# Key rows in two runs, values in eight pieces, the second unit's query rows ahead of the first weights, and nine warming products: one change to the opening of a fused attention and expert kernel

## The chip, the cores and the metric

The kernel runs on one core of one Trainium2 chip. The time is the device time of one execution in microseconds (us). Before the change, six runs gave a median of 487.77 us, from 487.45 to 488.29.

A core has five engines that matter here: TensorE (PE in the profile; its weight loads are PEld), VectorE (DVE), ScalarE (ACT), GpSimd (POOL) and SyncE (SP), which does nothing but issue DMAs. SPq and ACTq are the queues on which SP and ACT issue them.

## The reference

Attention first, with features that are products of two sketches of a row; then a mixture of four experts on its output. All is float32.

```
q, k, v: (4 batches, 4 heads, 1088 rows, 32)      S1, S2: (8, 32)
phi(x) = outer(S1 x, S2 x)                         # 64 features per row
kv = sum_s phi(k_s) v_s^T ;  z = sum_s phi(k_s)
attn = phi(q) kv / (phi(q) z + 1e-6)
x = attn, laid out as (4*1088, 4 heads * 32) = (4352, 128)
p = domain_probs / sum(domain_probs)               # (4352, 4)
out = sum_e p[:, e] * (relu(x @ w1[e]) @ w2[e])    # w1: (4,128,1024), w2: (4,1024,128)
```

The sum over the key rows runs over all 1088 of a batch and head, so the order in which they are taken is free, as long as keys and values are taken in the same order.

## The kernel before, in words

**Tiles.** A batch's k lies in SBUF as kn, 128 partitions by 1088 numbers: partition 32h+i holds 34 consecutive rows of head h, 32 numbers each. VectorE turns it in 32x32 blocks into kT, nine key tiles of 128 rows (the last is half full): `key_turn` (L326) turns tiles 0 to 3 with r = 0, 4 to 7 with r = 1, the half tile with r = 2. Before the change a tile of r = 0 takes its four groups of rows 8 rows apart, from the whole length of the partition's line. v comes as vn in four pieces of 1 KB runs, one for each group of 32 partitions, and two small ones for the half tile (`load_v`, L101); ScalarE copies it into vx (`value_copy`, L335). Query rows of a batch are worked on in units; those of batch 0 are 128, 448 and 512 rows, so the second unit is columns 128 to 575 of qn.

**Order.** All instructions are written out by hand in the order of the code; each engine takes its own in that order. `start()` (L674 on) does the first unit: `key_turn` for tiles 0 and 1, for 2 and 3, for r = 1 and r = 2 (VectorE), the query turn, the key products with the sketches (`key_project`, L344), ScalarE's copies of them and of v, feature products on VectorE and GpSimd, `key_sum` (72 products on TensorE), then the first unit's attention. The second unit's query turn (128x256 and 128x192) stands on VectorE ahead of `key_divide`. Then TensorE goes over the steps (L976): four steps per expert, each a first product (xT with w1, `first`, L775) and, two steps later, a second product (hidden units with w2, `second`, L831). Steps 0 to 3 need w1 of expert 0, steps 4 to 7 w1 of expert 1, and so on. Steps of the first 128 rows are short; from about 30 us on TensorE has long products.

**Warming.** `keep_warm(11)` (L192) puts eleven bfloat16 products of constants, 128x512, at TensorE's head; they are used for nothing.

**Loads.** All loads but one go through SP, in this order: S2, k of batch 0 (L99), the first 128 query columns, v (L105 four times, L110 twice), the other 960 query columns, w1 of expert 0 (L130), domain_probs in three and the ends' in two (L151, L156), w2 of expert 0 (L133), then w1 and w2 of experts 1, 2, 3. S1 goes through ACT. The framework gives the DMAs of all queues eight semaphores in turn, so an issue waits until the DMA eight places before it in the program has landed; w1 of expert 0, for instance, waits for the first query columns. Later batches are loaded by `load_batch` (L118) at step 5 and inside `front`, ahead of stores of y to DRAM (L609).

Of the kernel before, what the change touches and what calls it, by code (L numbers as in the profile page):

```python
# [8 lines left out]
F32 = mybir.dt.float32  # L9
# [3 lines left out]
ACTF = mybir.ActivationFunctionType  # L13
# [3 lines left out]
def _ap(t, p0: int, np_: int, off: int, free):  # L17

    p = list(t.ap)[0]
    return bass.AP(t.tensor, t.offset + p0 * p[0] + off, [[p[0], np_]] + [list(d) for d in free])  # L20
# [3 lines left out]
def kernel(  # L24
# [24 lines left out]
    nc = tc.nc  # L49

    P = 128
    HP = 64
    B, H, S, D = q.shape
# [3 lines left out]
    G = S // 32  # L57
# [8 lines left out]
    UNITS = [[P, 448, 512], [512, 320, 256], [448, 512, P], [384, 320, 384]]  # L66
# [6 lines left out]
    cpool = ctx.enter_context(tc.tile_pool(name="const", bufs=1))  # L73
# [10 lines left out]
    def psum(pool, tag):  # L84
        return pool.tile([P, 512], F32, tag=tag, name=tag)


    def load_rows(src, b, name, part=slice(0, S)):

        d = kn if name == "kn" else qn  # L90
        if b not in d:
            d[b] = lpool.tile([P, S], F32, tag=name, bufs=2, name=name)
        c, n = part.start, part.stop - part.start
        base = src.offset + b * H * S * D
        if name == "qn" and b == B - 1:
            for c, n, t in ((0, (G - 4) * D, 0), ((G - 4) * D, 4 * D, S - P)):
                nc.sync.dma_start(d[b][:, c : c + n], bass.AP(src.tensor, base + t * D, [[S * D, H], [n, 32], [1, n]]))
        else:
            nc.sync.dma_start(d[b][:, part], bass.AP(src.tensor, base + c, [[G * D, P], [1, n]]))  # L99

    def load_v(b):  # L101
        t = lpool.tile([P, H * NT * D], F32, tag="vn", name="vn")
        base = v.offset + b * H * S * D
        for a in range(4):
            nc.sync.dma_start(  # L105
                _ap(t, 32 * a, 32, 0, [[8 * D, H], [1, 8 * D]]),
                bass.AP(v.tensor, base + 8 * a * D, [[G * D, 32], [S * D, H], [1, 8 * D]]),
            )
        for a in range(2):
            nc.sync.dma_start(  # L110
                _ap(t, 32 * a, 32, 1024, [[D, H], [1, D]]),
                bass.AP(v.tensor, base + (32 + a) * D, [[G * D, 32], [S * D, H], [1, D]]),
            )
        return t

    kn, qn, vn = {}, {}, {}

    def load_batch(b):  # L118
        load_rows(k, b, "kn")
        vn[b] = load_v(b)  # L120
        load_rows(q, b, "qn")
# [7 lines left out]
    def load_w1(e):  # L129
        nc.sync.dma_start(w1_sb[:, e, :], w1[e])  # L130

    def load_w2(e):
        nc.sync.dma_start(w2_sb[:, e], w2[e].rearrange("(f p) d -> p f d", p=P))  # L133

    load_rows(k, 0, "kn")
    load_rows(q, 0, "qn", slice(0, P))
    vn[0] = load_v(0)


    warm = nc.const_aps.tensor(1.0, (P, 512), BF16)  # L140

    idle = cpool.tile([P, 1], F32, name="idle")
    nc.scalar.activation(idle[:, :], nc.const_aps.tensor(1.0, (P, 1), F32), ACTF.Identity)
    dp = cpool.tile([P, G, E], F32, name="dp")

    ends = cpool.tile([P, 2, E], F32, name="ends")
    e_sum = cpool.tile([P, 2, 3], F32, name="e_sum")
    load_rows(q, 0, "qn", slice(P, S))
    load_w1(0)
    for p0, n, g0, m, t in ((0, 96, 0, G, 0), (96, 32, 0, G - 4, 3 * S), (96, 32, G - 4, 4, B * S - P)):  # L150
        nc.sync.dma_start(  # L151
# [3 lines left out]
    for i, t, g in ((0, 0, G), (1, B * S - P, 4)):  # L155
        nc.sync.dma_start(  # L156
            ends[:, i, :], bass.AP(domain_probs.tensor, domain_probs.offset + t * E, [[g * E, 32], [1, 4 * E]])
        )
    load_w2(0)
    for e in range(1, E):  # L160
        load_w1(e)
        load_w2(e)
# [23 lines left out]
    def keep_warm(n):  # L186

        for _ in range(n):
            wp = psum(ps_h, "h")
            nc.tensor.matmul(wp[:, :], warm[:, 0:P], warm[:, :], start=True, stop=True)  # L190

    keep_warm(11)  # L192


    turn = [0]
# [130 lines left out]
    def key_turn(b, r, t0=0, n=4):  # L326
        if r < 2:
            nc.vector.transpose(
                _ap(kT, 0, P, 512 * r + P * t0, [[P, n], [32, 4], [1, 32]]),
                _ap(kn[b], 0, P, P * r + 32 * t0, [[32, n], [8 * D, 4], [1, 32]]),  # L330
            )
        else:
            nc.vector.transpose(kT[:, 1024:S], kn[b][:, 1024:S])
# [98 lines left out]
    def keys(b):  # L432
        for r in range(3):
            key_turn(b, r)
            yield
        kf = []
        for gi, (pool, tag) in enumerate(((ps_f, "f"), (ps_n, "den"), (ps_n, "num"))):
            kf.append(psum(pool, tag))
            key_project_wide(b, gi, kf[gi])
            if gi:  # L440
                key_add(b, gi - 1, kf[gi - 1])
            yield
        for _ in value_copy(b):
            pass
        for t0, n in ((0, 4), (4, 5)):
            if t0:
                key_add(b, 2, kf[2])
            for p in range(2):
                for x in range(2):
                    key_product(b, t0, n, p, x, nc.vector)  # L450
                    yield
        yield
        yield
        kv = psum(ps_f, "f")
        for p in range(2):
            key_sum(b, p, kv)
            yield
        key_blocks(b, kv)
        yield
# [214 lines left out]
    def start():  # L674
# [4 lines left out]
        for t0 in (0, 2):  # L679
            key_turn(b, 0, t0, 2)  # L680
        for r in (1, 2):
            key_turn(b, r)
# [366 lines left out]
```

## Time and profile before

| | us |
|---|---|
| median of six runs | 487.77 |
| profiled execution | 489.03 |
| its span, first to last instruction | 487.2 |
| time around the span | 1.83 |
| TensorE busy | 481.9 (99%) |
| VectorE busy | 320.9 (66%) |
| ScalarE busy | 246.6 (51%) |
| GpSimd busy | 229.9 (47%) |

A line of the chain of waits reads: start, length, what ran. A line of a timeline reads: start, length, engine, source line, operation, tile written <- tile read, shape, number of instructions merged, and in brackets the idle time before them with what ended it. A line of stages reads: from:to, its length, then each engine's busy time with its number of instructions, the granted TensorE clock, the busy share of the DMA engines and GB/s. A line of DMA issues reads: what, queue, operation, number, KB each, median us from the start of the issue to landing.

### The profile page before, as it was taken

The page shows a single profiled execution, that of the slowest core. Times are in us where ns is not written, and L with a number is a line of the kernel's source. Part 1 is how long each engine was busy: PE and PEld are TensorE (multiplying, and loading weights), DVE is VectorE, ACT ScalarE, POOL GpSimd, SP SyncE. Part 2 cuts the span into 40 slices and gives each one's busy share as a digit, 9 for nine tenths or more (in the row PEclk, how much of TensorE's full clock was granted, in tenths as well). Part 3 has the DMA queues.
Part 4 walks back from the last instruction along what each step waited for, and adds up shares of the span by engine and source line. Part 5 has one row for each costly group of instructions (what it writes and reads, how often), then busy time and mean ns, then how long its engine had stood idle before and what let it go on. Part 6 is the DMA issues. An engine that isn't in the chain of part 4 may idle for free.

```text
span 487.2 us, 11377 instructions
## 1 busy us (share of the span) xinstructions
PE 481.9 (99%) x4551; PEld 363.2 (75%) x4551; DVE 320.9 (66%) x759; ACT 246.6 (51%) x496; POOL 229.9 (47%) x270
## 2 busy tenths in 40 slices
PE   9999999999999999999999999999999999999997
PEld 6865666667777777777777777677777777999997
DVE  6759766585766658476776766668674666665642
ACT  4264464455554456355445545435455545566651
POOL 5172654425445445415455444424555445555571
PEclk9999999999999999999999999999999999999999
DMA  7991041111003123021103100021101200120000
GB/s 218 281 277 32 13 132 39 49 50 46 8 1 114 24 69 93 1 86 24 40 1 129 24 12 2 1 86 24 34 0 56 50 1 0 44 51 8 15 3 18
DMA packets 37772, 26.25 MB, mean 54 GB/s; under 512 B 24824, under 2 KB 34520, under 8 KB 37208
## 3 DMA queue, kind: packets, MB, share of 16 engines
q1 hardware_dynamic: 37704, 25.53, 18.6%
q8 instruction: 36, 0.59, 0.5%
q14 instruction: 16, 0.13, 0.1%
q10 hardware_dynamic: 16, 0.00, 0.0%
HBM read 21.28 MB, written 4.24 MB: 52 GB/s over the span
## 4 chain that ended last, share of the span: by engine, by line
PE 96%; DMA 2%; SPq 1%; issue 0%; DVE 0%
PE h L202 49%; PE o L202 41%; PE f L202 3%; PE den L202 2%; DMA w_sb<-in_moe_w_dram 2%; DMA vn<-in_v_dram 1%; PE num L202 0%; SPq L105 0%; SPq L156 0%; SPq L99 0%; SPq L133 0%; SPq L125 0%; DVE end L856 0%
## 5 line engine op out<-in xcount | busy, mean ns | idle before, releaser
L202 PE MATMUL h<-xT,w_sb 128*64 128x512 f32 (+5 forms) x1424 | 298.9, 491 | 1.2 <-DMA w_sb<-in_moe_w_dram 1.2
L786 DVE SCALAR_TENSOR_TENSOR hid<-h,hid 128x256 f32<-128x256 f32 (+6 forms) x432 | 203.8, 472 | 143.3 <-ACT hid L817 134.9
L817 ACT ACTIVATE hid<-h 128x512 f32<-128x512 f32 (+3 forms) x288 | 158.3, 550 | 192.5 <-PE h L202 146.2
L202 PE MATMUL o<-hid,w2s 128*64 128x256 f32 (+3 forms) x1152 | 223.9, 355 | 0.0
L202 PEld LDWEIGHTS h<-xT,w_sb 128*64 128x64 f32 x1424 | 146.5, 137 | 51.4 <-issue 7.5
L202 PE MATMUL o<-hid,w_sb 128*64 128x256 f32 (+3 forms) x864 | 183.7, 355 | 0.0
L202 PEld LDWEIGHTS o<-hid,w2s 128*64 128x64 f32 x1152 | 132.3, 137 | 28.8
L930 POOL TENSOR_TENSOR ev<-yz,sh 64x256 f32<-64x256 f32 (+3 forms) x72 | 48.6, 675 | 159.9 <-ACT sh L933 157.2
L202 PEld LDWEIGHTS o<-hid,w_sb 128*64 128x64 f32 x864 | 100.6, 137 | 24.9 <-issue 5.8
L918 POOL TENSOR_TENSOR yz<-ev 128x512 f32<-128x512 f32 (+3 forms) x36 | 41.8, 1160 | 60.5 <-ACT ev L921 60.3
L930 POOL TENSOR_TENSOR ct<-ev 128x512 f32<-128x512 f32 (+3 forms) x36 | 42.5, 1181 | 2.8
L930 POOL TENSOR_TENSOR total<-total,ct 128x512 f32<-128x512 f32 (+3 forms) x27 | 31.9, 1182 | 2.1
L930 POOL TENSOR_TENSOR ct<-ct,gate 128x512 f32<-128x512 f32 (+3 forms) x27 | 31.8, 1176 | 2.1
L501 DVE TENSOR_TENSOR qp<-qa,qb 64x512 f32<-64x512 f32 (+5 forms) x44 | 30.0, 683 | 1.0
L920 ACT COPY ev<-o 128x512 f32<-128x512 f32 (+3 forms) x36 | 19.4, 538 | 12.8 <-PE o L202 12.3
L202 PE MATMUL o<-w_sb,hid 128*64 128x128 f32 x256 | 21.4, 273 | 0.0
L921 ACT COPY ev<-o 128x512 f32<-128x512 f32 (+3 forms) x36 | 19.4, 538 | 2.0
L202 PEld LDWEIGHTS o<-w_sb,hid 128*64 128x64 f32 x256 | 17.2, 137 | 1.6 <-issue 0.9
L809 ACT ACTIVATE hid<-h 128x256 f32<-128x256 f32 x23 | 8.4, 384 | 19.3 <-PE h L202 18.9
L391 DVE TENSOR_TENSOR kp<-fs 128x256 f32<-128x256 f32 (+1 forms) x24 | 16.7, 698 | 0.1
L933 ACT COPY sh<-yz 64x256 f32<-64x256 f32 (+3 forms) x36 | 13.7, 380 | 1.6 <-POOL yz L918 0.8
L202 PEld LDWEIGHTS den<-kvx,qp 128*64 128x64 f32 x240 | 12.3, 137 | 2.6 <-issue 0.5
(129 smaller groups left out, 247.0 us busy)
## 6 DMA issues: line engine op xcount, KB each, us to landing
w_sb<-in_moe_w_dram SPq DMA_DIRECT2D x8, 512.0 KB, 7.8
gate<-gates SPq DMA_DIRECT2D x4, 1024.0 KB, 4.6
kn<-in_k_dram SPq DMA_DIRECT2D x4, 544.0 KB, 7.3
vn<-in_v_dram SPq DMA_DIRECT2D x16, 128.0 KB, 3.5
gate<-gates SPq DMA_DIRECT2D x2, 896.0 KB, 6.2
qn<-in_q_dram SPq DMA_DIRECT2D x2, 544.0 KB, 3.9
out_dram<-ob SPq DMA_DIRECT2D x16, 64.0 KB, 2.0
qn<-in_q_dram SPq DMA_DIRECT2D x2, 480.0 KB, 4.0
```

The costliest lines, as they stand in the source:

```text
L202: nc.tensor.matmul(out(s), weights(s), moving(s), **flags)
L391: eng.tensor_tensor(out=_ap(kps[b], 0, P, 256 * t0 + P * p + 64 * x, [[256, n], [32, 2], [R, 4], [1, R]]), in0=_ap(src, 0, P, off + 4 * x, ...
L501: nc.vector.tensor_tensor(out=qp[p][64 * x : 64 * x + 64, 0:n], in0=qa[64 * p : 64 * p + 64, 0:n], in1=qb[64 * p : 64 * p + 64, 0:n], op=A ...
L786: nc.vector.scalar_tensor_tensor(out=out, in0=src, scalar=0.0, in1=in1, op0=ALU.max, op1=ALU.subtract)
L809: nc.scalar.activation(hd[:, 0 : 2 * n], hp[:, 0 : 2 * n], ACTF.Relu)
L817: nc.scalar.activation(hd[:, n * j : n * j + n], hp[:, 0:n], ACTF.Relu)
L918: add = lambda out, in0, in1, op=ALU.add: nc.gpsimd.tensor_tensor(out=out, in0=in0, in1=in1, op=op)
L920: nc.scalar.copy(_ap(ev, 0, P, 0, [[2 * w, 2], [1, w]]), _ap(a0, 0, P, 0, two))
L921: nc.scalar.copy(_ap(ev, 0, P, w, [[2 * w, 2], [1, w]]), _ap(a1, 0, P, 0, two))
L930: add = lambda out, in0, in1, op=ALU.add: nc.gpsimd.tensor_tensor(out=out, in0=in0, in1=in1, op=op)
L933: nc.scalar.copy(sh[HP:P, 0:w], yz[0:HP, 0, 0:w])
```

## The change

Key tiles 0 to 3 are made of the first 16 rows of each partition's line and tiles 4 to 7 of the next 16, so each of them needs only one half of the line; k of batch 0 comes in two loads, columns 0 to 511 and 512 to 1087. v comes in eight pieces of 512-byte runs, four for each half, and the two small ones, for every batch. For batch 0 the first 128 query columns and one piece of v are issued on ACT, behind the activation `idle`, which moves ahead of the loads. Of the other query columns, the second unit's 448 stay ahead of w1 of expert 0, now behind all of v; the last 512 move behind w2 of expert 0. Nine warming products instead of eleven.

SP's order in batch 0 is now: S2, k (512 columns), k (576), v x7, small v x2, q (448), w1 of expert 0, domain_probs x3, ends x2, w2 of expert 0, q (512), w1 of expert 1, w2 of expert 1 and so on. Of the seven pieces of v on SP, the fifth waits for k's first load, the sixth for its second, the seventh for the query columns issued on ACT.

```diff
-    def load_rows(src, b, name, part=slice(0, S)):
+    def load_rows(src, b, name, part=slice(0, S), engine=nc.sync):
...
-            nc.sync.dma_start(d[b][:, part], bass.AP(src.tensor, base + c, [[G * D, P], [1, n]]))
+            engine.dma_start(d[b][:, part], bass.AP(src.tensor, base + c, [[G * D, P], [1, n]]))
...
-        for a in range(4):
-            nc.sync.dma_start(
-                _ap(t, 32 * a, 32, 0, [[8 * D, H], [1, 8 * D]]),
-                bass.AP(v.tensor, base + 8 * a * D, [[G * D, 32], [S * D, H], [1, 8 * D]]),
-            )
+        for r in range(2):
+            if b == 0 and r:
+                load_rows(q, 0, "qn", slice(0, P), nc.scalar)
+            for a in range(4):
+                (nc.scalar if b == 0 and r and a == 0 else nc.sync).dma_start(
+                    _ap(t, 32 * a, 32, P * r, [[8 * D, H], [1, P]]),
+                    bass.AP(v.tensor, base + (16 * r + 4 * a) * D, [[G * D, 32], [S * D, H], [1, P]]),
+                )
...
-    load_rows(k, 0, "kn")
-    load_rows(q, 0, "qn", slice(0, P))
-    vn[0] = load_v(0)
-    warm = nc.const_aps.tensor(1.0, (P, 512), BF16)
     idle = cpool.tile([P, 1], F32, name="idle")
     nc.scalar.activation(idle[:, :], nc.const_aps.tensor(1.0, (P, 1), F32), ACTF.Identity)
+    for part in (slice(0, 512), slice(512, S)):
+        load_rows(k, 0, "kn", part)
+    vn[0] = load_v(0)
+    warm = nc.const_aps.tensor(1.0, (P, 512), BF16)
...
-    load_rows(q, 0, "qn", slice(P, S))
+    load_rows(q, 0, "qn", slice(P, P + UNITS[0][1]))
     load_w1(0)
...
     load_w2(0)
+    load_rows(q, 0, "qn", slice(P + UNITS[0][1], S))
     for e in range(1, E):
...
-    keep_warm(11)
+    keep_warm(9)
...
-                _ap(kn[b], 0, P, P * r + 32 * t0, [[32, n], [8 * D, 4], [1, 32]]),
+                _ap(kn[b], 0, P, 512 * r + 32 * t0, [[32, n], [P, 4], [1, 32]]),
```

More of the change, by code (lines that the diff above doesn't have):

```diff
@@ L133, in load_w2 @@
         nc.sync.dma_start(w2_sb[:, e], w2[e].rearrange("(f p) d -> p f d", p=P))
-    load_rows(k, 0, "kn")
-    load_rows(q, 0, "qn", slice(0, P))
+    idle = cpool.tile([P, 1], F32, name="idle")
+    nc.scalar.activation(idle[:, :], nc.const_aps.tensor(1.0, (P, 1), F32), ACTF.Identity)
+    for part in (slice(0, 512), slice(512, S)):
+        load_rows(k, 0, "kn", part)
     vn[0] = load_v(0)
     warm = nc.const_aps.tensor(1.0, (P, 512), BF16)
-    idle = cpool.tile([P, 1], F32, name="idle")
-    nc.scalar.activation(idle[:, :], nc.const_aps.tensor(1.0, (P, 1), F32), ACTF.Identity)
     dp = cpool.tile([P, G, E], F32, name="dp")
```

## The prediction

> **What bounds the kernel now.** I read the page first, then the waits of TensorE, the chain of waits of the first 31 us, the stages there, and last SP's timeline. The page and TensorE's waits up to 30 us:
>
> ```profile
> PE 481.9 (99%) x4551; PEld 363.2 (75%) x4551; DVE 320.9 (66%) x759; ACT 246.6 (51%) x496; POOL 229.9 (47%) x270
> PE   9999999999999999999999999999999999999997
> ```
>
> ```profile
> PE h L202 <- DMA w_sb<-in_moe_w_dram: 1.2, 1, 1.2
> PE h L190 <- PEq L1033: 0.8, 1, 0.8
> ```
>
> TensorE is full in every slice but the last. The change touches the opening alone, and there TensorE has one real wait: 1.2 us for a weight load. So a gain at the head counts only if it isn't given back at that load. The chain of waits of the first 31 us shows which load it is:
>
> ```profile
> 2.09 0.43 SPq L105
> ...
> 2.57 0.43 SPq L105
> ...
> 7.88 0.68 SPq L156
> ...
> 9.23 0.43 SPq L133
> ...
> 9.70 7.81 DMA w_sb<-in_moe_w_dram
> ...
> 17.65 0.66 PE h L202 x8
> ```
>
> SP's queue (SPq) issues w2 of expert 0 at 9.23, then at 9.70 the load that lands 7.81 later, at 17.5. That is the next in SP's order, w1 of expert 1, which step 4 needs. The chain runs through SP and this load and not through k or the key products: those have slack. Whether SP or the DMA engines hold the load up, the stages tell (the last two are of TensorE alone):
>
> ```profile
> 9.75:11.25 1.50, 1.50 (x59) 1.50 (x56) 1.43 (x6) 0.14 (x1) 1.21 (x7) 1.00 0.39 80
> 13.00:14.00 1.00, 1.00 (x20) 0.50 (x18) 0.86 (x4) 0.00 (x0) 0.58 (x3) 1.00 0.71 126
> 14.00:15.00 1.00, 1.00 (x42) 1.00 (x38) 0.97 (x5) 0.28 (x1) 0.00 (x0) 1.00 0.90 273
> 16.00:17.00 1.00, 0.49 (x10) 0.24 (x6) 0.97 (x5) 0.04 (x1) 0.00 (x0) 1.00 1.22 322
> 17.00:18.00 1.00, 0.35 (x6) 0.38 (x8) 0.96 (x5) 0.00 (x0) 0.17 (x1) 1.00 0.93 339
> ```
>
> ```profile
> 5.70:6.10 0.40, 0.35 (x7) 1.00 1.11 183
> 6.10:6.50 0.40, 0.40 (x19) 1.00 1.23 205
> ```
>
> From 9.75 to 11.25 the DMA engines are 0.39 busy at 80 GB/s, while SP issues one DMA after another: there SP is the limit. At 13 to 14, when w1 of expert 1 gets going, the rate is 126 GB/s; full flow is some 330 (mean of 322 and 339). SP's own timeline:
>
> ```profile
> 5.15 0.35 SPq L99 DMA_DIRECT2D qn<-in_q_dram  x1
> 5.55 0.43 SPq L130 DMA_DIRECT2D w_sb<-in_moe_w_dram  x1
> 9.70 1.54 SPq L130 DMA_DIRECT2D w_sb<-in_moe_w_dram  x1
> 11.77 1.26 SPq L130 DMA_DIRECT2D w_sb<-in_moe_w_dram  x1
> ```
>
> [...]
>
> **Part 1, the head.** k's first 256 KB should land as xT's 256 KB from DRAM do, 2.5 us after the issue (k whole: 3.9), so at 1.21 + 2.5 = 3.7. VectorE is then still at the sketches until 4.24 and turns the first two tiles at 4.24 to 4.65, not from 5.16. The sketch copies end on GpSimd at 4.76, and nine warming products at 0.44 (4.85 for eleven) end at 4.75. So TensorE's key products start at about 4.85 instead of 5.75. They won't run at full pace at once: at 5.70 to 6.10 seven came in 0.35 us, then 19 in 0.40, so 20 per us against some 48 to 55, and that change of pace need not come earlier. From 4.85 to 6.1 that is 25 products where there were 7; 18 more, at 50 per us, are 0.4 us. I take 0.4, between 0 (pace changes later, two warming products fewer) and 0.9 (all of the earlier start). TensorE would then stand before w1 of expert 1 at 16.5 - 0.4 = 16.1. Two of ACT's issues (0.43 to 0.58 each by S1's) lie in its 1.5 us wait before the sketch copies, and cost nothing unless they pass it. The new strides of `key_turn` move the same 32x32 blocks: nothing.
>
> **Part 2, SP's queue up to w1 of expert 1.** Issues stand 0.475 apart (2.09, 2.57). k in two and four pieces of v fill SP to 3.95. The fifth piece waits for k's first load (3.7): at 3.99. The sixth waits for the second, which ends where k ended, 5.15. The seventh waits for the query columns, issued on ACT at about 2.85 and landing 2.0 to 2.6 later (rows of 64 and 128 KB), by 5.5: no wait. From 5.15 on SP is never late for a landing, only for itself: two pieces of v, two small ones, q's 448 columns, w1 of expert 0, six at 0.475, to 8.0; domain_probs three times, 1.45 less 0.5 of waits there and three gaps, 1.1; ends 1.3: w2 of expert 0 at 10.4, not 9.23. That is 1.2 later. Behind it q's 512 columns take the long issue (1.5), to 12.45, and w1 of expert 1 is issued at 12.5, not 9.70. What queues behind on SP, the other weights, moves with it; w2 of expert 1 has 0.6 us of slack (needed at 19.86, landed 19.3), and the later ones no less, so they add nothing of their own.
>
> **Part 3, its landing.** Low end: alone in the queue it would take what q's 544 KB take later, 3.9, so 16.4. High end: 17.5, plus 1.2 as w2 before it is later, plus 256 KB of q now ahead of it at 330 GB/s, 0.8: 19.5. I take off what the slow start at 13 to 16 lost against 330 GB/s (0.6, 0.2 and 0.1 us by 126, 273, 298), since q's columns now stand in that place and the weights follow in full flow: 18.6. It is nearer the high end because w2, the stream ahead of it, cannot come earlier than SP issues it.
>
> **Part 4, v, q and later batches.** v's last piece leaves SP at 5.6 and lands within 2.6, at 8.2; ScalarE's second copy was at 8.9. The small ones land by 8.9 against a copy at 9.4. The second unit's query rows, issued at 7.05 with 2.5 to 4 to land, meet a turn at 11.2. Covered, up to 0.3 us at worst, and this too would lie ahead of the wait at 16.1. Four more issues a batch, 1.9 us of SP, have 20 us before the next store (26.6 to 59.0) and as much later: nothing.
>
> **The sum.** TensorE goes on at 18.6 instead of 17.5: +1.1 us. The head's 0.4 only lengthens the wait, from 1.2 to 2.5. On the profiled execution, 489.03, that gives 490.1; it lies 1.26 above the median, so on the median 488.9.
>
> [...]
>
> **The rivals.**
>
> *Not slower: the weights are as late as before.* If q's columns fit in the hole at 9.75 to 14 and the two pieces of k and eight of v bring all else earlier, w1 of expert 1 lands between 16.6 and 18.4: -1.0 to +0.9, centre 488.0. For it: bytes ahead of it are the same as before, and v's 1 KB pieces flowed badly (213 GB/s at 5 to 6). Against: SP's count above.
>
> *Faster: the load comes before TensorE needs it.* It decides where w1 of expert 1 lands by 16.5; then the wait of 1.2 and up to 0.9 of the head are saved: 485.7 to 486.8, middle 486.3. For it: the head's 0.9 is real time on TensorE. Against: its issue at 12.5 leaves 3.9 us, what a lone load takes.
>
> *Slower by more: TensorE's pace falls in the longer wait.* 1.17 us of idling left the next products at full pace; 2.5 to 3.4 is untried here. The slow pace lasted to 6.1 from 0.78; losing half of at most that, 2.7, is the upper price: 489.0 to 491.6. [...]
>
> **How the numbers follow.** 0.2% (1 us) is what a measurement of this kernel tells from no change. The forecast (load at 18.5 to 19.5, +1.0 to +2.0) has 0.45, the weights as late as before 0.33, faster 0.15, the fall in pace 0.07. Slower: 0.45 + 0.07, less a little at the border, 0.51; same 0.33; faster 0.16. The forecast's own range is 488.7 to 489.8. The whole range runs from 486.8 (the load just in time) to 490.0, and leaves out most of the faster case and the pace case, some 0.18.
>
> **What would show it.** Key products near 4.85; SP issuing w2 of expert 0 near 10.4 and w1 of expert 1 near 12.5; that load landing near 18.6; TensorE idle before step 4 by 2.5 us; DMA engines mostly idle at 6 to 8, when SP issues small pieces. I'd be wrong if SP's issues of 64 KB pieces are shorter than 0.43, if the sixth piece of v doesn't wait for k, or if the load, once issued, lands within 4 us.

## The result and the profile after

The changed kernel took 492.04 us, the median of 20 runs (489.54 to 495.27); the kernel before, on the same chips, 487.89 (40 runs). The ratio is 1.0082, 95% interval 1.0071 to 1.0093: slower by 4.2 us, outside the predicted range. The profiled execution took 492.41, with a span of 490.6 against 487.2 before.

Two lines of the page's tenths (TensorE's busy share and its granted clock), and the two longest of TensorE's waits up to 40 us (total, times, longest), of the changed kernel:

```profile
PE   8799999999999999999999999999999999999997
PEclk9899999999999999999999999999999999999999
```

```profile
PE o L208 <- DMA w_sb<-in_moe_w_dram: 1.3, 1, 1.3
PE h L208 <- DMA w_sb<-in_moe_w_dram: 2.2, 1, 2.2
```

Two weight waits stand where there was one of 1.2. The second slice (12.3 to 24.5 us) also has a lower granted clock, which it had not before. SP's timeline shows why the weights are late (start, length, line, tile):

```profile
8.03 2.15 SPq L156 DMA_DIRECT2D dp<-in_moe_domain_probs_dram  x3
10.22 1.31 SPq L161 DMA_DIRECT2D ends<-in_moe_domain_probs_dram  x2
11.57 0.43 SPq L137 DMA_DIRECT2D w_sb<-in_moe_w_dram  x1
12.04 0.58 SPq L99 DMA_DIRECT2D qn<-in_q_dram  x1
12.67 0.43 SPq L134 DMA_DIRECT2D w_sb<-in_moe_w_dram  x1
```

w2 of expert 0 goes out at 11.57 instead of 9.23, w1 of expert 1 at 12.67 instead of 9.70. The stages say that the DMA engines had room before that: at 6 to 7 us, when SP issues small pieces, they are 0.41 busy, and at 12 to 13 us 0.19; at 18 to 19 us, with the weights under way, they are full. At 12 to 13 us, 152 of the 217 packets they move are under 512 bytes, the gates' small loads ahead of w2. Whether SP's issue time or these packets keep w2 from flowing there, no run tells apart: the gates' loads were only moved whole. The same view shows the clock in its column before the last two (the last two are DMA share and GB/s):

```profile
6.00:7.00 1.00, 0.84 (x28) 0.87 (x30) 1.00 (x5) 0.24 (x1) 0.62 (x2) 1.00 0.41 111
...
12.00:13.00 1.00, 1.00 (x10) 0.29 (x10) 0.90 (x3) 0.00 (x0) 0.00 (x0) 1.00 0.19 36
18.00:19.00 1.00, 0.00 (x0) 0.00 (x0) 0.94 (x3) 0.00 (x0) 0.00 (x0) 1.00 1.19 327
20.00:21.00 1.00, 1.00 (x23) 1.00 (x20) 0.05 (x1) 0.38 (x1) 0.00 (x0) 0.95 1.15 331
22.00:23.00 1.00, 1.00 (x13) 1.00 (x11) 0.93 (x2) 0.04 (x1) 0.00 (x0) 0.50 1.03 374
24.00:25.00 1.00, 1.00 (x20) 1.00 (x17) 0.00 (x0) 0.38 (x1) 0.00 (x0) 0.84 1.25 290
```

The clock is 0.95 in the stage from 20, 0.50 in the three stages after it, and 0.84 in the one from 24. So it fell at 20.9 and came back at 24.3 (20.90 and 24.31 in the trace's clock records): 3.4 us at half, with 13 products in a stage of 1 us where there were 23. The chain of waits before, then after, from step 4 to the first products that write `den`:

```profile
17.65 0.66 PE h L202 x8
...
22.24 0.44 PE h L202 x8
22.68 0.35 PE den L202 x12
```

```profile
12.67 6.76 DMA w_sb<-in_moe_w_dram
...
19.56 0.66 PE h L208 x8
...
22.87 0.85 PE o L208 x8
...
25.82 0.44 PE h L208 x8
26.25 0.35 PE den L208 x12
```

Step 4 begins at 19.56 instead of 17.65: 1.9 late, through the load issued at 12.67. Then groups of eight take 0.85 instead of 0.44. At the products that write `den`, the changed kernel is 26.25 - 22.68 = 3.57 behind, so the fall in clock has added 3.57 - 1.91 = 1.66, half of its 3.4 us; at the end the spans differ by 490.6 - 487.2 = 3.4. All that is lost is lost by 26 us; the later batches lose nothing.

The 20 times of the changed kernel fall into groups by the mean granted clock of the whole execution:

| mean clock | runs | median us |
|---|---|---|
| 0.999 to 1.000 | 7 | 490.06 |
| 0.996 to 0.997 | 9 | 492.14 |
| 0.993 | 4 | 493.7 |

A stretch of 3.4 us at half clock in 490 lowers the mean by 0.5 x 3.4 / 490 = 0.0035; the groups fit none, one and two such stretches. Between the groups lie some 2.1 us (492.14 - 490.06) for one and 3.7 for two. The trace gives one fall 1.66, so the groups may differ in the length of their waits as well. Without any, the kernel is still 490.06 - 487.89 = 2.2 slower.

### The profile page after: what moved, and what is told of

It reads as the page before. It is cut to its first block, busy times and chain, and to the rows that moved or that the text cites. A ratio compares the mean times of both kernels' runs of the same rounds, so it can differ in the third digit from the quotient of the medians.

```text
span 490.6 us, 11401 instructions
## 1 busy us (share of the span) xinstructions
PE 482.6 (98%) x4549; PEld 364.3 (74%) x4549; DVE 320.7 (65%) x759; ACT 246.5 (50%) x496; POOL 229.7 (47%) x270
## 2 busy tenths in 40 slices
DMA packets 40364, 26.25 MB, mean 54 GB/s; under 512 B 25112, under 2 KB 36984, under 8 KB 39800
## 4 chain that ended last, share of the span: by engine, by line
PE 95%; DMA 2%; SPq 2%; issue 0%; DVE 0%
PE h L208 49%; PE o L208 40%; PE f L208 3%; PE den L208 2%; DMA w_sb<-in_moe_w_dram 1%; DMA kn<-in_k_dram 1%; PE num L208 0%; SPq L156 0%; SPq L99 0%; SPq L161 0%; SPq L114 0%; SPq L109 0%; SPq L134 0%; SPq L137 0%; SPq L129 0%
## 5 line engine op out<-in xcount | busy, mean ns | idle before, releaser
L926 ACT COPY ev<-o 128x512 f32<-128x512 f32 (+3 forms) x36 | 19.4, 539 | 12.6 <-PE o L208 12.3
L208 PE MATMUL o<-w_sb,hid 128*64 128x128 f32 x256 | 22.4, 283 | 1.3 <-DMA w_sb<-in_moe_w_dram 1.3
L208 PEld LDWEIGHTS den<-kvx,qp 128*64 128x64 f32 x240 | 12.3, 137 | 2.5 <-issue 0.5
```

The costliest lines, as they stand in the source:

```text
L208: nc.tensor.matmul(out(s), weights(s), moving(s), **flags)
L926: nc.scalar.copy(_ap(ev, 0, P, 0, [[2 * w, 2], [1, w]]), _ap(a0, 0, P, 0, two))
```

## The experiments

Two theories were put on trial. A: the weights are late for their place in SP's queue; TensorE waits, and in the longer waits its clock falls. B: the loss lies elsewhere, in the new strides or the eight pieces of v of later batches, or in the bytes to be moved, whatever their order on SP. The chain of waits above has already spoken against the later batches.

**Filling the waits (e1_fill).** On the changed kernel, constant products, used for nothing, are put into the two waits, so that TensorE is not idle in them; the loads stay.

```diff
+    def fill_warm(n):
+        wp = psum(ps_h, "h")
+        for _ in range(n):
+            nc.tensor.matmul(wp[:, :], warm[:, 0:P], warm[:, :], start=True, stop=True)
...
+        if i == LA + 2:
+            fill_warm(8)
         if i < len(steps):
...
+        if i == LA:
+            fill_warm(4)
         if i >= LA:
             second(i - LA)
```

> The changed kernel with idle work for TensorE: 4 constant products (bfloat16, 128x512) ahead of step 0's second products and 8 ahead of step 4. Theory A (the loss is two waits for weight loads, w2 of expert 0 and w1 of expert 1, and a fall of TensorE's clock that the second wait brings): the loads land as before at 16.1 and 19.4, the clock stays 1.000, and only the clock's part is given back: 490.0 to 490.5, from 492.0. Rival B (the loss lies in the later batches, whose v now comes in eight pieces of 512-byte runs and whose keys are turned by other strides): 492.0 or a little more, and a clock of 1.000 would not help.

Measured: 490.76 (490.24 to 491.21, 7 runs), ratio 1.0047, interval 1.0030 to 1.0063, below that of the changed kernel. The clock was 0.999 or 1.000 in all seven runs, where 13 of 20 had shown a fall. TensorE's timeline of this kernel (idle time before a group would stand in brackets):

```profile
15.84 1.05 PE L201 MATMUL h<-const-bfloat16-1.0 128*128 128x512 bf16 x3
17.84 1.92 PE L201 MATMUL h<-const-bfloat16-1.0 128*128 128x512 bf16 x8
19.69 0.66 PE L213 MATMUL h<-xT,w_sb 128*64 128x128 f32 x8
```

Step 4 is as late as before, 19.69, but its products go on at full pace. With the idling filled no run had a fall, so in this kernel the fall in clock comes from the idling. The lateness of step 4 is not the load's here. The chain of waits of this kernel runs through the constant products:

```profile
17.91 1.85 PE h L201 x8
19.76 0.59 PE h L213 x8
```

By the trace's semaphores the load had landed at 18.56, so step 4 could have begun near 18.7, and the filling itself holds it up by some 1.0 us. What it gives back, 492.04 - 490.76 = 1.3 us of the median, is therefore the fall less the price of the filling, and the 2.7 that are left against its own runs of before (488.10) are the late loads and the filling together. A had 490.0 to 490.5, without that price.

**SP's order mended, one load at a time (e2_gates_behind, e3_q_behind, e7_both_behind).** On the changed kernel, the five loads for the gates go behind w1 of expert 1; or the 512 query columns go behind w2 of expert 1; or both.

```diff
     load_w1(0)
-    for p0, n, g0, m, t in ((0, 96, 0, G, 0), (96, 32, 0, G - 4, 3 * S), (96, 32, G - 4, 4, B * S - P)):   # e2, e7
...
     load_w2(0)
-    load_rows(q, 0, "qn", slice(P + UNITS[0][1], S))    # e3, e7
     load_w1(1)
+    for p0, n, g0, m, t in ((0, 96, 0, G, 0), (96, 32, 0, G - 4, 3 * S), (96, 32, G - 4, 4, B * S - P)):   # e2, e7
...
     load_w2(1)
+    load_rows(q, 0, "qn", slice(P + UNITS[0][1], S))    # e3, e7
     for e in range(2, E):
```

> The changed kernel with the five loads of domain_probs and ends issued behind w1 of expert 1 instead of ahead of w2 of expert 0; nothing else. Theory A (SP's issue time holds up the weights): w2 of expert 0 is issued near 8.0 instead of 11.6, w1 of expert 1 near 9.7 instead of 12.7 and lands near 16.0 to 16.5; the clock stays 1.000; 486.3 to 487.5. A variant, that bytes and not issues decide (the five loads carry 70 KB): the load lands less than 0.5 earlier, 491 to 492. Rival B (later batches): 491 to 492.

> The changed kernel with the last 512 query columns behind w2 of expert 1 instead of ahead of w1 of expert 1. Theory A: w2 of expert 0 unchanged (lands 16.1), w1 of expert 1 earlier by the 256 KB and one issue, 0.7 to 1.0, so at 18.5; the second wait is 1.3 instead of 2.2; 490.0 to 491.2, with the clock falling in fewer runs. Rival B: 492.

> Both of the above: domain_probs and ends behind w1 of expert 1, and the last 512 query columns behind w2 of expert 1. Theory A: w1 of expert 1 lands near 15.3 to 16.0, no later than TensorE comes to step 4 (15.8); the head's gain of 0.66 and the former wait of 1.17 show in full: 485.8 to 486.5, faster than both kernels. Rival B: 490 to 491.

Measured: gates' loads behind, 489.25 (ratio 1.0017, 1.0006 to 1.0028); query columns behind, 490.45 (1.0041, 1.0025 to 1.0056); both, 488.60 (1.0006, 0.9993 to 1.0019). Each mend brings time back, as A has it, but the first and the last of the three stay some 2 us above what was expected of them. The lines below are of TensorE's timeline with the gates' loads behind, and then with both behind:

```profile
16.18 0.66 PE L210 MATMUL h<-xT,w_sb 128*64 128x128 f32 x8
...
21.57 0.66 PE L210 MATMUL h<-xT,w_sb 128*64 128x128 f32 x8 [1.59 <-DMA w_sb<-in_moe_w_dram]
```

```profile
20.48 0.66 PE L210 MATMUL h<-xT,w_sb 128*64 128x128 f32 x8 [0.65 <-DMA w_sb<-in_moe_w_dram]
...
22.93 0.57 PE L210 MATMUL den<-kvx,qp 128*64 128x66 f32 x12 [0.46 <-DVE qp L509]
```

Step 4 no longer waits; step 8 does, for w1 of expert 2, by 1.59 and 0.65. The wait moved one load down the queue. What holds that load is not only the issues ahead of it. With the gates' loads behind, the chain reads:

```profile
8.34 6.34 DMA qn<-in_q_dram
14.70 6.73 DMA w_sb<-in_moe_w_dram
```

SP issues w1 of expert 2 at 14.70, when the DMA eight places before it, the 512 query columns, has landed (14.68): the eight semaphores taken in turn. The trace of the changed kernel shows the same: its loads on SP and ACT go round eight semaphores, and the fifth and sixth of SP's pieces of v, on those of k's two loads, go out at 4.00 and 5.30, once k has landed (3.99 and 5.28). With both behind, SP waits 0.9 us at the same issue, for w1 of expert 1. Five small loads moved behind big ones bring a big one into the eighth place. With both loads moved, a second wait appears too, for VectorE's query features (qp). VectorE's timeline of this kernel shows why:

```profile
17.76 0.25 DVE L287 TENSOR_SCALAR e_sum<-e_sum 128x2 f32<-128x2 f32 x1 [1.46 <-POOL e_sum L278]
```

VectorE takes the gates' quotients ahead of those features, and now stands 1.46 us for GpSimd's sums of the late gates' loads.

**One part of the change alone, on the kernel before (e5_v8, e4_q_split).** v in eight pieces, keys as they were; or the 512 query columns behind w2 of expert 0, v as it was.

```diff
-        for a in range(4):                                  # e5
+        for r in range(2):
+            for a in range(4):
...
-    load_rows(q, 0, "qn", slice(P, S))                      # e4
+    load_rows(q, 0, "qn", slice(P, P + UNITS[0][1]))
...
     load_w2(0)
+    load_rows(q, 0, "qn", slice(P + UNITS[0][1], S))        # e4
```

> The kernel before with one part of the change: v in eight pieces of 512-byte runs (keys' order as before, so each 1 KB run is cut in two), all on SP. Theory A (more, smaller DMAs hold up SP, whose issues cost 0.475 each and wait for the DMA eight places before): w2 of expert 0 issued 1 to 2 later than 9.2, w1 of expert 1 later by as much, 489.0 to 490.5, with or without a fall of the clock. Rival C (the 256 KB of q and not v's pieces made the change slow): 487.8 to 488.3.

> The kernel before with one part of the change: the second unit's 448 query columns ahead of w1 of expert 0, the last 512 behind w2 of expert 0. Theory A: the bytes ahead of w1 of expert 1 are the same and one issue is added that takes the place of the long one behind w2; the load lands 0.3 to 0.8 later, 488.0 to 488.8. Rival C: 489 to 490.

Measured: eight pieces 488.99 (1.0027, 1.0017 to 1.0038); the query columns split 488.66 (1.0011, 1.0002 to 1.0021); before in the same set 487.86. Both lie at or in their ranges. SP's timeline with eight pieces:

```profile
2.09 3.75 SPq L106 DMA_DIRECT2D vn<-in_v_dram  x8
...
10.55 1.16 SPq L134 DMA_DIRECT2D w_sb<-in_moe_w_dram  x1
11.75 0.58 SPq L131 DMA_DIRECT2D w_sb<-in_moe_w_dram  x1
```

Four more pieces are 1.9 us of SP (3.75 against 1.86), and w2 of expert 0 goes out at 10.55. The pieces' runs are also half as long (512 bytes instead of 1 KB), and no run varied that alone. The two medians differ from their runs of before by 1.1 and 0.8; together that is 1.9 of the 2.2 us which the whole change costs at full clock. This sum supports A; it does not show that the parts add. The profiled execution of the split one was its fastest run (487.61) and lists no weight wait, so where its 0.8 comes from isn't shown.

**The kernel before with SP's order mended (e6_before_gates_behind, e8_before_both_behind).** The same moves on the kernel before; in the second, the query columns are split as well and 512 of them go behind w2 of expert 1.

```diff
-    load_rows(q, 0, "qn", slice(P, S))                      # e8
+    load_rows(q, 0, "qn", slice(P, P + UNITS[0][1]))        # e8
     load_w1(0)
-    for p0, n, g0, m, t in ((0, 96, 0, G, 0), (96, 32, 0, G - 4, 3 * S), (96, 32, G - 4, 4, B * S - P)):
...
     load_w2(0)
     load_w1(1)
+    for p0, n, g0, m, t in ((0, 96, 0, G, 0), (96, 32, 0, G - 4, 3 * S), (96, 32, G - 4, 4, B * S - P)):
...
     load_w2(1)
+    load_rows(q, 0, "qn", slice(P + UNITS[0][1], S))        # e8
```

> The kernel before with the five loads of domain_probs and ends issued behind w1 of expert 1. Theory A: w1 of expert 1 is issued near 7.5 and lands near 14 to 15; TensorE doesn't wait there; what binds next is w1 of expert 2, as in the changed kernel with the same edit; 487.3 to 488.0. If the waits of most runs of the kernel before are smaller than the 1.2 of its profiled one, whose time lies 1.2 above the median, there is little to gain: 487.6.

> The kernel before with the five loads behind w1 of expert 1 and the last 512 query columns behind w2 of expert 1. Theory A: no wait for a weight load is left; 487.2 to 487.7, level with or just ahead of the kernel before, since its head is 0.66 later than the changed one's. If the waits for weights were no part of the time in most runs of the kernel before: 487.9.

Measured: 487.69 (1.0002, 0.9993 to 1.0011) and 487.83 (1.0008, 0.9991 to 1.0024): no change. There is no weight wait in either profile, and still nothing is gained. The next pair says why; in the first of the two there is also a wait of 0.56 for VectorE's qp, as with both behind above. One of the eleven runs of the second took 491.98 at a mean clock of 0.997, so with a fall; that run was not traced, and what brought the fall on is not known.

**Both kernels looked at a second time (e0_before_again, e0_after_again).** No edit.

> The kernel before, profiled a second time. If the wait of 1.17 for w1 of expert 1 is an accident of the first profiled execution (489.03, 1.15 above the median), this one shows a wait of 0 to 0.5, a span of 486.0 to 486.5 and a time near 487.9. If it is steady, the wait is again near 1.2 and the span 487.

> The changed kernel, profiled a second time. Theory A: again one wait of 1 to 1.5 before step 0's second products and one of 2 to 2.5 before step 4. [...]

Measured: before 487.31, after 489.79, one run each. The wait for w1 of expert 1 in the kernel before is 0.23 here, not 1.17:

```profile
13.11 1.65 PE L202 MATMUL h<-xT,w_sb 128*64 128x64 f32 x48
...
16.32 0.66 PE L202 MATMUL h<-xT,w_sb 128*64 128x128 f32 x8 [0.23 <-DMA w_sb<-in_moe_w_dram]
```

The first profile of before was of an execution 489.03 - 487.31 = 1.72 slower. Of this, 1.33 lies ahead of step 4 (17.65 against 16.32), whose load landed later: TensorE came there 0.39 later (first products of expert 0 at 13.50) and waited 0.94 longer. In the second profile there is next to nothing to gain at this load, which fits the two experiments before it. In the changed kernel the second profile shows no fall in clock, weight waits of 0.22, 0.88 and 0.41 (1 to 1.5 and 2 to 2.5 were expected), and a wait that is not in the first, on VectorE:

```profile
11.66 0.45 DVE L494 STREAM_TRANSPOSE qT<-qn 128x256 f32<-128x256 f32 x1 [0.88 <-DMA qn<-in_q_dram]
```

The second unit's query rows came late; VectorE's turn of them stands ahead of `kvz`, for which TensorE waited 1.0 us. The first products of expert 0 began at 13.96, later than in the kernel before (13.11). Step 4 began at 18.26 against 16.32, and TensorE still stood 0.88 before it for its load: without a fall, too, the weights set the pace.

**Reordered to take out every weight wait (e9_after_reordered, e10_gates_behind_w2).** On the changed kernel: gates' loads behind w1 of expert 1 (e9) or behind w2 of expert 1 (e10), 512 query columns behind w2 of expert 2, and the gates' quotients two steps later so that VectorE does not wait in them. The loop over experts is written out.

```diff
     load_w2(0)
     load_w1(1)
+    for p0, n, g0, m, t in ((0, 96, 0, G, 0), (96, 32, 0, G - 4, 3 * S), (96, 32, G - 4, 4, B * S - P)):   # e9
...
     load_w2(1)
+    for p0, n, g0, m, t in ((0, 96, 0, G, 0), (96, 32, 0, G - 4, 3 * S), (96, 32, G - 4, 4, B * S - P)):   # e10
...
     load_w1(2)
     load_w2(2)
+    load_rows(q, 0, "qn", slice(P + UNITS[0][1], S))
...
-            if i == 2:
+            if i == 4:
                 gate_quotients()
```

> The changed kernel with the five loads behind w1 of expert 1, the last 512 query columns behind w2 of expert 2, and the gates' quotients on VectorE at step 4 instead of 2, so that they don't stand ahead of the second unit's products. Theory A: no wait for w1 of expert 1 or 2 is left and the head's 0.66 shows: 487.1 to 487.7, ahead of the kernel before by 0.2 to 0.8. If weights bound by bytes still come late, or the head's gain is lost elsewhere: 488.0 to 488.6.

> This is the changed kernel with SP's order k, v, q (448 columns), w1 and w2 of expert 0, w1 and w2 of expert 1, domain_probs and the ends' loads, w1 and w2 of expert 2, q (512 columns), w1 and w2 of expert 3, and the gates' quotients at step 4. The profile of the kernel with the gates' loads between w1 and w2 of expert 1 had one weight wait left, 0.86 us for w2 of expert 1, issued at 12.85 behind 3.0 us of gates' loads; its median was 488.25. Theory A (weights wait for their place in SP's queue, and every wait there reaches the end): w2 of expert 1 is issued near 9.8, no weight wait above 0.3 us is left, and the time falls by 0.5 to 0.9, to 487.3 to 487.8, the level of the kernel before or a little under it. Theory B (the weights are bound by bytes, and the wait only moves to the next load): a wait of 0.5 us or more stands at w1 or w2 of expert 2, and the time stays at 488.0 to 488.6.

Measured: 488.25 (1.0010, 1.0000 to 1.0020; before 487.54) and 488.38 (1.0007, 0.9998 to 1.0016; before 488.10). SP's timeline and TensorE's waits up to 40 us of the second:

```profile
8.44 0.58 SPq L134 DMA_DIRECT2D w_sb<-in_moe_w_dram  x1
9.06 0.43 SPq L137 DMA_DIRECT2D w_sb<-in_moe_w_dram  x1
9.54 4.07 SPq L159 DMA_DIRECT2D dp<-in_moe_domain_probs_dram  x3
14.99 0.43 SPq L134 DMA_DIRECT2D w_sb<-in_moe_w_dram  x1
```

```profile
PE h L199 <- PEq L1042: 0.8, 1, 0.8
PE den L211 <- DVE qp L510: 0.3, 1, 0.3
PE den L211 <- DVE kvz L423: 0.2, 1, 0.2
```

No weight wait is listed any more, and the loss is gone within the interval (that of the last run reaches 0.8 us): the new strides and the pieces of v cost nothing that can be told from that once the weights are in time. So far A holds. Its times, 487.1 to 487.7 and 487.3 to 487.8, do not; both lie where the other theory put them, though the last kernel has no wait of the 0.5 that B asked for. (The profile of the first of the two still had a wait of 0.86 to 18.76. It is put down to VectorE there, but w2 of expert 1, issued at 12.85, landed at 18.62.) And no version beats the kernel before. Its step 4 starts at 15.99 against 16.32 in the second profile of before, 0.33 ahead; at about 30 us it is 0.49 behind. TensorE's timeline shows two places for this 0.82:

```profile
19.04 0.61 PE L211 MATMUL o<-w_sb,hid 128*64 128x128 f32 x8
19.80 0.66 PE L211 MATMUL h<-xT,w_sb 128*64 128x128 f32 x8
...
21.48 0.32 PE L211 MATMUL num<-kvx,qp 128*64 128x66 f32 x4
22.08 0.57 PE L211 MATMUL den<-kvx,qp 128*64 128x66 f32 x12 [0.29 <-DVE qp L510]
```

From 19.04 to 19.80 is 0.76 where steps stand 0.44 apart: 0.32, at the first step of expert 2. No releaser is given, but by the trace's semaphores its weights, issued at 14.99, landed at 19.66, and step 4 in the chains above also starts some 0.14 after its load: it is a small weight wait. From 21.48 to 22.08 is 0.60 where the kernel before has 0.11: 0.49, for VectorE's qp. The chain of waits leads from there back to the gates' loads, the last of which lands at 18.00:

```profile
14.36 3.64 DMA ends<-in_moe_domain_probs_dram
```

The head's lead is gone within 6 us, and both parts of the loss come from the order of SP's loads: the gates' loads are now late for VectorE, and w1 of expert 2 stands behind their issues. The wait has moved on here too.

## Why the prediction was wrong, point by point

Three steps failed. The fall in pace was given 0.07 for a wait of 2.5 us, a length that the profile of before did not show; it came after 2.24, in 13 of 20 runs, and lifted the median from 490.06 (runs without a fall) to 492.04. In the landing of w1 of expert 1, the delay of w2 ahead of it was put at 1.2 and was 2.34. And the sum was moved from the profiled execution to the median by a constant, 1.26, much of which, by a second profile, came from the very load whose wait the change replaces. That the weights are late on SP's queue, the mechanism of the forecast, held.

- **Part 1, the head.** Within its range between the first two profiles. Key products began at 4.68 (4.85 predicted), and the first products of expert 0 at 12.84 instead of 13.50: 0.66 in the range of 0 to 0.9. But the start varies: 13.96 in the second profile of the changed kernel, 13.11 in that of the kernel before, so the 0.66 is in part luck. How much an early start is worth depends on when TensorE's pace rises, and that lay between 3.83 and 6.59 in four profiles. Stages of TensorE alone (products in brackets), first of the changed kernel, then of the last experiment:

```profile
4.80:5.20 0.40, 0.40 (x18) 1.00 1.26 205
```

```profile
4.80:5.20 0.40, 0.40 (x10) 1.00 1.28 216
...
6.80:7.20 0.40, 0.40 (x22) 1.00 0.51 131
```

  The first has 18 products in 0.4 us at 4.8 already, the second 10 there and 22 only from 6.8 on, though both started their key products at 4.7. The trace's clock records put the start of full clock at 3.83 and 6.59 in these two, and at 6.09 and 4.74 in the two profiles of the kernel before. "That change of pace need not come earlier" held: it comes when it comes.
- **Part 2, SP's queue.** The issue of w1 of expert 1 was right, 12.67 against 12.5, but by two errors that cancel. The gates' five loads took 3.5 us (8.03 to 11.53) and not 1.1 + 1.3, so w2 of expert 0 went out at 11.57 and not 10.4. And q's issue behind it took 0.58 and not 1.5. The stage of 9.75 to 11.25 was read as one issue after another; SP's timeline has a single one there (9.70 to 11.24). No run shows 1.5 as a steady price of this place: the issue behind w2 of expert 0 took 1.54 in the first profile of the kernel before and 0.49 in the second. Long issues stood elsewhere in the row too, at the gates' loads (2.15 for three, and 4.07 in the last experiment) or at w2 itself (1.16 with eight pieces of v); what sets them is not shown.
- **Part 3, the landing.** 19.43 and not 18.6: near the top end, 19.5. The mis-sized term is the 1.2 for w2, which went out 2.34 later (11.57 against 9.23) behind the gates' loads. The other two terms, 0.8 for q's bytes less 0.9 for the slow start, came to -0.1 in the sum; measured, 1.91 - 2.34 = -0.43 is left for them. So taking something off for the slow start was right, and too little. It did not go away altogether: the engines were 0.19 busy at 12 to 13.
- **Part 4.** The strides, the eight pieces of later batches and their issues were covered, as said (3.57 behind at 26 us, 3.4 at the end). The second unit's query rows, "covered, up to 0.3 us at worst", cost 0.88 us of VectorE in one of two profiles; TensorE then stood for weights anyway, so little or none of it reached step 4. And w2 of expert 0 was counted only as a place in the queue: that TensorE waits for it too was left out, 1.28. Step 4 starts when its own load has landed (19.56 and 19.43), so this wait adds nothing to the time; it shortens the one after it.
- **The sum.** Step 4 at 19.56 is +1.9 on the profiled execution, where 1.1 was forecast. The second error is the base. The sum was made on the profiled execution, 490.1, and 1.26 taken off to reach the median; but the second profile of before shows that this execution was long in good part by the very wait that the change replaces (step 4 is 1.33 of the 1.72 us later there). Not shifted, 490.1 is the median that the changed kernel has at full clock, 490.06; that the two agree so closely is luck, since with the measured 1.9 in place of 1.1 the sum would be 490.9.
- **The rival that came: "TensorE's pace falls in the longer wait".** It had 0.07, and came in 13 of 20 runs. Its price of 0 to 2.7 covers one fall (1.66 in the trace, 2.1 between the groups) and is too low for two (3.7); even its own range ended at 491.6. Its 0.07 was the author's estimate; the profile of before had one wait to judge by, 1.17 us, after which groups of eight went on at 0.44. In the trace the fall came 1.34 us after the wait of 2.24 had ended (20.90 against 19.56), with the products under way, and lasted 3.41. What makes it come in some runs and not in others, no run shows.
- **SP's issue time**, on which the forecast rests, was no small thing: four more issues of 64 KB on SP are 1.9 us (3.75 against 1.86), and v in eight pieces alone, runs half as long included, made the kernel 1.1 us slower. In the changed kernel the engines were 0.41 busy at 6 to 7 us, while SP issued small pieces.

## What to carry to other kernels

On a queue with more, smaller loads ahead of a critical one, count the issues first, and with them the loads that an issue must wait for; here the bytes said little, with the DMA engines 0.41 busy at 6 to 7 us and 0.19 at 12 to 13. Where a profiled execution is above the median, find the wait that put it there before making a sum on it, since a change to that wait cannot be moved to the median by a constant. An idle stretch of 2.24 us on TensorE was followed here by 1.66 us more, lost in clock, and 13 of 20 runs of the changed kernel had such a fall: fill it with constant products, or take the wait out, and take out the next one behind it too before counting a gain.

## What the hardware showed that was not expected

- The fall in clock is one stretch of 3.41 us at 0.50 in the trace's clock records, begun 1.34 us after a wait of 2.24 us, and it is or is not there from run to run of the same kernel (mean clock 1.000, 0.997 or 0.993).
- ScalarE's queue ran two DMA issues during the engine's own table load, ahead of the activation that stands before them in the program. They went out at 1.42 and 1.81 instead of the 2.85 reckoned with. The timeline of ScalarE in the changed kernel:

```profile
1.35 1.28 ACT L141 ACT_TABLE_LOAD   x1 [1.35 <-PEq L1039]
1.42 0.36 ACTq L99 DMA_DIRECT2D qn<-in_q_dram  x1
1.81 0.44 ACTq L109 DMA_DIRECT2D vn<-in_v_dram  x1
2.64 0.20 ACT L141 ACTIVATE idle<-const-float32-1.0 128x1 f32<-128x1 f32 x1
```

- Three issues of domain_probs took 1.4 us with eight pieces of v, 2.15 in the changed kernel and 4.07 behind two w2 loads. What sets this is open: no run here varied it alone.
